# Outputs in the buffers of the relu results, inverse decays in the buffers of the inputs, and a new written-out order: gated linear attention and an MLP mixer on one core

## The chip, the core and the metric

The kernel runs on one core of a Trainium2 chip. A core has TensorE (PE; its weight loads are shown apart as PEld), VectorE (DVE), ScalarE (ACT), GpSimd (POOL) and SyncE (SP), and sixteen DMA engines that move data between HBM and the core's memory. Each engine works through its own list of instructions in order and waits where a semaphore tells it to. The metric is the device time of one launch in microseconds (us), as a median of runs.

## What is computed

The inputs are `q`, `k`, `v`, `alpha` of 4 batches x 8 heads x 768 steps x 48, and four weight matrices of a mixer, all fp32. First comes an attention with a decaying state, then, on its result `x` (4 x 768 x 384), a token mixer and a channel mixer:

```python
for t in range(S):
    state = alpha[:, :, t, :, None] * state + np.einsum('bhd,bhe->bhde', k[:, :, t], v[:, :, t])
    y[:, :, t] = np.einsum('bhd,bhde->bhe', q[:, :, t], state)
# x = y with the heads side by side
h  = np.maximum(x.transpose(0, 2, 1) @ w_tok1, 0.0) @ w_tok2
u  = x + h.transpose(0, 2, 1)
out = u + np.maximum(u @ w_ch1, 0.0) @ w_ch2
```

## The kernel before

**Attention.** The 768 steps of a batch are three chunks of 256; four batches make twelve chunks, numbered 0 to 11. For a chunk, `ld_at`, `ld_kt`, `ld_qt`, `ld_vt` load 384 KB each into buffers of the class `in` (L584). ScalarE takes logarithms (`ln`, L637; from chunk 3 on `P` on POOL or VectorE first, L628, then `ln1`, `lnP`), TensorE sums them (`cum`, `cumw`), and ScalarE makes the decay `E` (L683, L676) and its inverse `IE` (L687, L679). `qq` and `kk` (L700) multiply q by E and k by IE; from chunk 3 on `q0r` (L696) and `k0a` (L692) go ahead of them. `trq` and `trk` transpose them on TensorE (L712), and `evq`, `evk` evict the results; from chunk 6 on the transposes are DMAs of the SP queue, `dq` and `dk` (L725), with `pq` behind. `vb` casts v (L746 on VectorE and POOL, L745 on ScalarE), and `vs`, `ka`, `kb`, `kc` are half-tile copies at the same lines. `G` multiplies keys and queries in narrow blocks of 48 rows, `mask` (L770) keeps the causal half, `K` forms the state's increment, `s` or `sa` and `sm` (L837, L841, L844) update the state `ss`, `ia`, `ib` and `y` give the output, and `x` (L745, L746) evicts it. The two `hf` halves of a chunk are numbered 0 and 1: `mask1_2` is the second mask of chunk 2.

**Mixer.** For each batch `t1` (L878) and `ht` are the first token product and its relu, `t2` (L883) and `u` (L887) the second one and the sum with x. u is transposed into `ut`, in batch 0 by TensorE (`up`, L894) and an eviction, later by DMAs of the SP queue (`ux`, L729). `c1` (L902) is the first channel product, 24 blocks of three matmuls a batch, `rt` its relu (L873 on ScalarE, L875 on VectorE) into twelve buffers of 128 x 768 bf16. `c2` (L907) is the second, four quarters of three matmuls for each of six output tiles; `o` (L911, VectorE) adds u, and `st` (L624) stores 192 KB of fp32 to HBM, from the SP queue or from ScalarE's. In the last batch the tile 0 is cut into two half tiles (`0h0`, `0h1`).

**What sets the order.** `build` lists the steps with their buffers' classes; a fixed text, `ORDER`, names every step once in the order in which it is issued, with a last letter for its engine (t TensorE, s ScalarE, v VectorE, g POOL, y SP), and `BUFS` gives the buffer number of each value in the order of first use. Each engine gets its steps in this order and never passes one. Steps `f1_...` to `f12_...` are dummy matmuls that keep TensorE going at the start. `shared` (L732) makes POOL and VectorE take turns: a step marked `port` on one of them waits for the last such step on the other. `CLASSES` says how many buffers a class has: a step that writes a buffer waits until the last reader of what was in it is done, and for an output that reader is its store. Before the change, outputs have a class `o` of three buffers and IE one of two.

## Time and profile before

| what | before |
|---|---|
| median of 3 runs | 162.97 us (162.54 to 163.51) |
| span of the profiled execution, first to last instruction | 160.5 us |
| TensorE busy in the span | 154.6 us (96%) |
| VectorE, ScalarE, POOL busy | 114.9, 97.8, 80.8 us |
| read from HBM, written | 25.17 MB, 4.72 MB |

The profile is of one execution on the chip; the runs' times are of the whole launch, so 2.5 us of the median lie outside the span. The profiled execution has no time of its own in the records besides its span; 160.5 + 2.5 us stands for it. A row of the timeline has the start, the busy time, the engine, the line, the operation and how many of them were merged; in brackets stands how long the engine was idle before and what released it. A row of a group has busy time and the mean duration of one in ns, and then the idle time before them. A row of waits has the total, how often, and the longest. A row of a stretch has, for each of the five engines, its busy time and the number of its instructions, then the granted clock of TensorE, the share of the DMA engines and GB/s. "issue" is time in which an engine waited for nothing that the profile shows.

### The profile page before, as it was taken

The page shows a single profiled execution, that of the slowest core. Times are in us where ns is not written, and L with a number is a line of the kernel's source. Part 1 is how long each engine was busy: PE and PEld are TensorE (multiplying, and loading weights), DVE is VectorE, ACT ScalarE, POOL GpSimd, SP SyncE. Part 2 cuts the span into 40 slices and gives each one's busy share as a digit, 9 for nine tenths or more (in the row PEclk, how much of TensorE's full clock was granted, in tenths as well). Part 3 has the DMA queues.
Part 4 walks back from the last instruction along what each step waited for, and adds up shares of the span by engine and source line. Part 5 has one row for each costly group of instructions (what it writes and reads, how often), then busy time and mean ns, then how long its engine had stood idle before and what let it go on. Part 6 is the DMA issues. An engine that isn't in the chain of part 4 may idle for free.

```text
span 160.5 us, 3971 instructions
## 1 busy us (share of the span) xinstructions
PE 154.6 (96%) x1563; PEld 97.1 (60%) x1563; DVE 114.9 (72%) x206; ACT 97.8 (61%) x179; POOL 80.8 (50%) x94
## 2 busy tenths in 40 slices
PE   7999989999999999999999999999999999999992
PEld 2545565766667676666667666566567665665661
DVE  6099994979889787989969758795886762464222
ACT  3789999998899955897563583269832203343000
POOL 5205897695973649389778852699523000000000
PEclk9999999999999999999999999999999999999999
DMA  4999999999999999999989999989701235111133
GB/s 122 320 324 317 317 374 311 339 333 306 316 347 324 275 278 272 210 228 319 241 202 298 239 315 204 217 196 134 196 21 62 87 79 169 49 49 53 49 129 116
DMA packets 76130, 35.05 MB, mean 218 GB/s; under 512 B 70352, under 2 KB 74320, under 8 KB 76112
## 3 DMA queue, kind: packets, MB, share of 16 engines
q1 hardware_dynamic: 73808, 31.76, 74.1%
q10 hardware_dynamic: 2304, 3.05, 5.3%
q8 instruction: 12, 0.20, 0.5%
q14 instruction: 6, 0.05, 0.1%
HBM read 25.17 MB, written 4.72 MB: 186 GB/s over the span
## 4 chain that ended last, share of the span: by engine, by line
PE 61%; DMA 12%; DVE 6%; ACT 6%; SPq 6%; POOL 4%; issue 3%; DVEq 0%; POOLq 0%
PE ps L907 22%; PE ps L902 21%; PE ps L643 11%; DMA in<-in_v_dram 6%; SPq L584 6%; DMA out_dram<-o 4%; PE ps L878 3%; PE ps L883 2%; DMA ut<-u 2%; DVE pkk L700 2%; DVE gtm L770 1%; PE ps L712 1%; DVE rt L875 1%; POOL vb L746 1%; POOL pkq L700 1%
## 5 line engine op out<-in xcount | busy, mean ns | idle before, releaser
L907 PE MATMUL ps<-wc,rt 128*128 128x384 bf16 (+1 forms) x300 | 52.4, 319 | 0.0
L902 PE MATMUL ps<-ut,wc 128*128 128x384 bf16 x288 | 50.3, 326 | 0.1
L902 PEld LDWEIGHTS <-wc 128*128 128x128 bf16 x288 | 27.1, 98 | 17.9 <-DMA ut<-u 0.6
L907 PEld LDWEIGHTS <-rt 128*128 128x128 bf16 x300 | 27.8, 98 | 16.0
L873 ACT ACTIVATE rt<-ps 128x384 bf16<-128x384 f32 x47 | 21.4, 492 | 23.6 <-PE ps L902 23.3
L875 DVE TENSOR_SCALAR rt<-ps 128x384 bf16<-128x384 f32 x49 | 25.6, 551 | 9.1 <-PE ps L902 8.9
L770 DVE TENSOR_TENSOR gtm<-ps,mk 128x1024 bf16<-128x1024 f32 x24 | 28.5, 1218 | 3.1 <-PE ps L643 2.8
L911 DVE TENSOR_TENSOR o<-ps,u 128x384 f32<-128x384 f32 (+1 forms) x25 | 13.2, 536 | 12.6 <-PE ps L907 10.1
L700 POOL TENSOR_TENSOR pkk<-in,IE 128x768 bf16<-128x768 f32 x8 | 14.5, 1817 | 3.3 <-DVE ss L844 2.3
L745 ACT CAST x<-ps 128x384 bf16<-128x384 f32 x20 | 9.2, 479 | 11.1 <-PE ps L643 9.5
L887 DVE TENSOR_TENSOR u<-ps,x 128x384 bf16<-128x384 f32 x24 | 12.0, 550 | 3.1 <-PE ps L883 2.5
L746 POOL CAST vb<-in 64x384 bf16<-64x384 f32 (+1 forms) x14 | 8.3, 594 | 10.4 <-DMA in<-in_v_dram 4.7
L692 POOL TENSOR_TENSOR in<-in,in 128x384 f32<-128x384 f32 x8 | 8.0, 1000 | 10.5 <-DVE u L887 3.8
L643 PE MATMUL ps<-rt 128*128 128x512 bf16 (+1 forms) x29 | 12.1, 515 | 1.1 <-DVE rt L541 1.1
L745 ACT CAST vb<-in 64x384 bf16<-64x384 f32 (+1 forms) x18 | 11.4, 634 | 0.8 <-DMA in<-in_v_dram 0.3
L700 POOL TENSOR_TENSOR pkq<-in,E 128x768 bf16<-128x768 f32 x6 | 10.9, 1818 | 0.6 <-DMA tpk<-pkq 0.3
L878 PE MATMUL ps<-x,wt 128*128 128x384 bf16 x48 | 11.0, 325 | 0.0
L844 POOL TENSOR_TENSOR ss<-tmp,E 128x384 bf16<-128x384 f32 x10 | 8.3, 833 | 4.2 <-DVE in L628 3.9
L841 DVE TENSOR_TENSOR tmp<-ps,ss 128x384 f32<-128x384 f32 x16 | 8.8, 552 | 1.8 <-PE ps L643 0.6
L883 PE MATMUL ps<-ht,wt 128*128 128x384 bf16 x48 | 9.1, 326 | 0.0
L643 PE MATMUL ps<-vb,gtm 128*128 128x48 bf16 x192 | 8.2, 183 | 0.2 <-DVE gtm L770 0.2
L643 PE MATMUL ps<-tpq,tpk 48*64 48x128 bf16 (+1 forms) x288 | 7.9, 218 | 0.4 <-POOL tpq L746 0.3
(94 smaller groups left out, 207.6 us busy)
## 6 DMA issues: line engine op xcount, KB each, us to landing
in<-in_alpha_dram SPq DMA_DIRECT2D x12, 384.0 KB, 5.1
in<-in_v_dram SPq DMA_DIRECT2D x12, 384.0 KB, 5.6
in<-in_k_dram SPq DMA_DIRECT2D x12, 384.0 KB, 5.2
in<-in_q_dram SPq DMA_DIRECT2D x12, 384.0 KB, 5.5
in<-in_moe_w_ch_dram SPq DMA_DIRECT2D x12, 384.0 KB, 5.9
...
```

Source lines behind the costliest of these rows:

```text
L643: return self.pe.matmul(out, lhsT=lhsT, rhs=rhs, start=start, stop=stop, skip_group_check=True)
L700: self.shared(self.eng[e].tensor_tensor(self.t(dst)[:, :, h0:h1, 0:D], self.t(src)[:, h0:h1].rearrange("p h s d -> p s h d"), bass.AP(tens ...
L745: return self.act.copy(d, s)
L770: self.nc.vector.tensor_tensor(self.t(gtm)[:, hf, :, :], self.pair(gp).rearrange("p a (j t) -> p (a j) t", t=128), bass.AP(tensor=m.tensor ...
L873: self.act.activation(d, s, AF.Relu)
L875: self.nc.vector.tensor_scalar_max(d, s, 0.0)
L878: self.pe.matmul(self.bank(bank)[:, 0:HD], lhsT=self.wt1[:, kc, m * 128 : m * 128 + 128], rhs=self.t(x), start=(kc == 0), stop=(kc == NS - 1))
L883: self.pe.matmul(self.bank(bank)[:, 0:HD], lhsT=self.wt2[:, kc, i * 128 : i * 128 + 128], rhs=self.t(hts[kc]), start=(kc == 0), stop=(kc = ...
L887: self.nc.vector.tensor_tensor(self.t(u)[:, i % 3], self.bank(bank)[:, 0:HD], self.t(x), ALU.add)
L902: self.pe.matmul(self.bank(bank)[:, 0:HD], lhsT=self.wc1[:, kc, mc * 128 : mc * 128 + 128], rhs=self.t(ut)[:, 3 * half : 3 * half + 3, kc, ...
L907: self.pe.matmul(self.bank(bank)[:, 0 : cz - ca], lhsT=self.t(rts[mc][0])[:, i * 128 : i * 128 + 128], rhs=self.wc2[:, mc, ca:cz], start=( ...
L911: self.nc.vector.tensor_tensor(self.t(o)[:, ca:cz], self.bank(bank)[:, 0 : cz - ca], self.t(u)[:, i % 3, ca:cz], ALU.add)
```

## The change

The classes `IE` and `o` go. Their values keep their names but take buffers of `in` and `rt`, through `ALIAS`; `t` returns such a buffer as a flat tile (for IE) or as fp32 (for an output, 128 x 384 in the same bytes as 128 x 768 bf16). The number of bytes is the same. All of `ORDER` and `BUFS` is replaced, and with them the engine of some steps, the fillers and the place of the stores.

```diff
     def val(self, cls, name=""):
-        return Val(cls, name)
+        return Val(ALIAS.get(cls, cls), cls)
...
-    "in": 19,
-    "la": 2, "lf": 2, "E": 3, "IE": 2, "pkq": 2, "pkk": 3, "vb": 3,
-    "tpk": 4, "tpq": 2, "gtm": 2, "tmp": 2, "ss": 4, "kt": 1, "x": 9, "ht": 3, "u": 4, "ut": 2, "rt": 20, "o": 3,
+    "in": 21,
+    "la": 2, "lf": 2, "E": 3, "pkq": 2, "pkk": 3, "vb": 3,
+    "tpk": 4, "tpq": 2, "gtm": 2, "tmp": 2, "ss": 4, "kt": 1, "x": 9, "ht": 3, "u": 4, "ut": 2, "rt": 23,
 }
+ALIAS = {'o': 'rt', 'IE': 'in'}
...
     def t(self, v):
-        return self.T[v.cls][v.buf]
+        t = self.T[v.cls][v.buf]
+        if v.name == v.cls:
+            return t
+        if v.cls == "rt":
+            return t[:, :].bitcast(F32)
+        return t.rearrange("p h t d -> p (h t d)")
```

The beginning of the order, up to the first `c1`:

```diff
-ld_at1y ld_at0y ln1s ln0s f8_cumw1t f1_cumw1t cumw1t IE1s cumw0t IE0s ld_vt0y E0s vb0g vs0_0g vs1_0v ld_kt0y kk0v
-f8_trk0t f1_trk0t trk0t E1s ld_qt0y qq0v ka0s kb0s kc0v f1_trq0t trq0t ld_kt1y kk1v K0t evq0s s0_0v ld_vt1y vb1s
-f1_trk1t trk1t ld_at2y evk0v ln2s f2_G0_0t G0_0t ld_qt1y ka1g sa1_0v f4_cumw2t cumw2t mask0_0v vs0_1s kb1g kc1g vs1_1s
-K1t sm1_0g qq1v sa0_1v sm0_1v G1_0t ld_kt2y IE2s E2s trq1t evq1s ib0t mask1_0v f3_y1_0t y1_0t y0_0t evk1v G0_1t sa1_1v
-ld_qt2y x1_0s mask0_1v G1_1t ld_vt2y x0_0s vb2s kk2g trk2t kc2s ldw_wt10y qq2g cw_wt10s f2_ia1t ia1t mask1_1v evk2s
-trq2t ld_at3y vs1_2g ldw_wt11y evq2v ib1t y1_1t y0_1t vs0_2g ldw_wt21y sm1_1g P3g K2t sa0_2v sm0_2g x0_1s t1_0_0_0t
-f1_G0_2t G0_2t ldw_wt20y G1_2t cw_wt20g t1_0_1_0t mask0_2v x1_1s t1_0_1_1t ld_at4y ld_kt3y t1_0_1_2t lnP3s cum3t
-cw_wt11s IE3s ia2t y0_2t x0_2s t1_0_0_1t t1_0_0_2t E3s t1_0_0_3t mask1_2v t1_0_1_3t ib2t y1_2t ldw_wc14y t1_0_1_4t
-x1_2s t1_0_0_4t f1_t1_0_1_5t t1_0_1_5t ht_0_1v P4g cw_wt21s t1_0_0_5t ht_0_0s f3_t2_0_0t t2_0_0t t2_0_1t u_0_0v ln13s
-r13s ldw_wc13y t2_0_2t u_0_1v t2_0_3t u_0_2v t2_0_5t lnP4s t2_0_4t u_0_3v u_0_5v u_0_4v up_0_0t cw_wc14s cw_wc13s
-ldw_wc15y up_0_1t ld_qt3y k0a3g kk3g cum4t trk3t cw_wc15g ut_0_0v up_0_2t ut_0_2v ut_0_1s c1_0_11_0t c1_0_8_0t IE4s
...
+ld_kt0y ld_at0y ln0s f12_cumw0t f2_cumw0t cumw0t ld_at1y ln1s ld_qt0y E0s qq0v cumw1t IE0s kk0v IE1s E1s f2_trq0t
+trq0t evq0s ld_kt1y kk1v trk0t evk0v ld_at2y ln2s ld_qt1y kb0s qq1v f3_trk1t trk1t G1_0t evk1v ld_vt0y vb0s ka0g kc0g
+G0_0t cumw2t vs0_0s trq1t ld_vt1y vb1g vs1_0g mask0_0v mask1_0v ld_kt2y IE2s kk2v evq1s f4_K0t K0t E2s f1_G1_1t G1_1t
+vs0_1g s0_0v ib0t ka1v mask1_1v ld_qt2y sa1_0v qq2g y0_0t y1_0t f3_G0_1t G0_1t mask0_1v vs1_1s kb1s kc1s sm1_0g K1t
+sa0_1v trq2t trk2t x1_0s ia1t ldw_wt10y cw_wt10s x0_0s ldw_wt21y cw_wt21g evk2v evq2s y0_1t x0_1v f3_G0_2t G0_2t
+sm0_1g sa1_1v ib1t y1_1t ld_vt2y vb2s mask0_2v G1_2t kc2g t1_0_0_0t vs0_2s K2t ldw_wt11y ld_at3y x1_1s vs1_2s sm1_1g
+t1_0_0_1t ia2t sa0_2v cw_wt11g t1_0_0_2t mask1_2v t1_0_0_3t ld_qt3y ldw_wt20y ln13s t1_0_1_0t r13s t1_0_1_1t y0_2t
+ldw_wc15y sm0_2g ib2t y1_2t t1_0_1_2t t1_0_1_3t x0_2s t1_0_1_4t x1_2s t1_0_0_4t ldw_wc14y t1_0_0_5t P3g lnP3s
+t1_0_1_5t ht_0_1s cum3t ht_0_0v cw_wt20g t2_0_1t E3s u_0_1v t2_0_3t u_0_3v t2_0_0t u_0_0v t2_0_2t t2_0_5t cw_wc15s
+t2_0_4t up_0_0t cw_wc14s IE3s u_0_2v q0r3g qq3g up_0_1t trq3t u_0_5v u_0_4v up_0_2t ldw_wc13y ut_0_1v cw_wc13g ut_0_0s
+c1_0_9_0t evq3s c1_0_10_0t ld_kt3y k0a3v kk3g rt_0_9_0s ut_0_2v c1_0_10_1t rt_0_10_1v ld_vt3y vb3s vs0_3g kb3s ld_at4y
```

Its end, with the second channel product of the last batch:

```diff
-rt_3_9_0v rt_3_4_1s c1_3_5_1t st_1_0y c1_3_9_1t rt_3_9_1s st_2_3s c2_3_2_0t rt_3_5_1v rt_3_10_1v c2_3_2_1t c2_3_2_2t
-c2_3_2_3t c1_3_8_1t rt_3_8_1s o_3_2v c1_3_11_1t rt_3_11_1s c2_3_5_0t c2_3_5_1t rt_3_7_1v c2_3_5_2t c2_3_5_3t c2_3_3_0t
-c2_3_0h1_0t st_3_2s c2_3_0h1_1t c2_3_3_1t c2_3_0h1_2t c2_3_0h1_3t o_3_0h1v st_3_0h1s o_3_5v c2_3_1_0t st_3_5s
-c2_3_3_2t c2_3_3_3t c2_3_4_0t o_3_3v st_3_3y c2_3_4_1t c2_3_4_2t c2_3_4_3t o_3_4v c2_3_1_1t c2_3_1_2t c2_3_1_3t o_3_1v
-st_3_4s c2_3_0h0_0t c2_3_0h0_1t c2_3_0h0_2t c2_3_0h0_3t o_3_0h0v st_3_0h0y st_3_1s
...
+c1_3_7_0t rt_3_7_0v rt_3_5_0v rt_3_10_0v c1_3_9_0t rt_3_5_1v c1_3_3_0t rt_3_3_0s c1_3_0_0t o_2_1v c1_3_1_0t rt_3_1_0v
+c1_3_0_1t rt_3_0_1s st_0_1s c1_3_2_1t c1_3_11_0t c1_3_4_0t rt_3_4_0s c1_3_4_1t c1_3_8_1t c1_3_3_1t rt_3_0_0s
+c2_3_0h0_0t rt_3_2_1v rt_3_9_0v c1_3_6_0t rt_3_6_0v c2_3_2_0t rt_3_11_0v c2_3_0h0_1t c2_3_2_1t c2_3_0h0_2t c2_3_0h0_3t
+o_3_0h0v c2_3_2_2t c2_3_2_3t c2_3_1_0t c2_3_1_1t st_1_2y c2_3_1_2t c2_3_1_3t o_3_1v st_3_1y rt_3_3_1s rt_3_4_1s
+c2_3_5_0t rt_3_8_1s c2_3_4_0t c2_3_4_1t c2_3_4_2t c2_3_5_1t c2_3_4_3t o_3_4v st_3_4s c2_3_5_2t c2_3_5_3t st_2_2y
+st_2_0y o_3_5v st_3_5s o_3_2v st_0_3y c2_3_3_0t c2_3_3_1t c2_3_3_2t c2_3_0h1_0t st_3_2s st_2_4s st_2_1s c2_3_3_3t
+o_3_3v st_3_3y c2_3_0h1_1t c2_3_0h1_2t c2_3_0h1_3t st_3_0h0s st_2_5s o_3_0h1v st_3_0h1y
```

And the stretch of the new order between the token product and the channel product of batch 1:

```diff
+x1_5v t1_1_0_5t ht_1_0v t1_1_1_4t t1_1_1_5t c2_0_1_1t o_0_0v lnP6s cum6t ht_1_1s t2_1_2t u_1_2v t2_1_0t u_1_0v t2_1_5t
+t2_1_1t t2_1_3t u_1_1v IE6s u_1_3v ld_kt8y ln17s t2_1_4t u_1_4v r16s u_1_5v c2_0_1_2t c2_0_4_0t P8g lnP8s E6s
+c2_0_4_1t c2_0_4_2t c2_0_4_3t k0a6g P7g kk6g kb6v ld_qt6y q0r6v k0a8v ld_vt6y vb6s vs0_6v qq6v ld_qt7y ux_1_0y lnP7s
+ux_1_1y r17s q0r7g c2_0_1_3t o_0_1v o_0_4v cum7t IE7s cum8t E8s IE8s E7s c1_1_2_0t rt_1_2_0s c1_1_9_0t rt_1_9_0s
+c1_1_11_0t rt_1_11_0s kk8v c1_1_9_1t rt_1_9_1s c1_1_4_0t ld_vt7y ld_qt8y qq7v c1_1_11_1t rt_1_11_1v c1_1_0_0t
```

95 lines of the change are left out of this document (44 added, 51 removed), and 22 rows, old and new, of the table BUFS.

## The prediction

> **What bounds the kernel now.** I read the page first (span and busy shares), then the busy time of the stretch from 32 us on, then what TensorE's weight loads (PEld, which run ahead of the matmuls and so meet every wait first) waited for in it.
>
> ```profile
> span 160.5 us, 3971 instructions
> PE 154.6 (96%) x1563; PEld 97.1 (60%) x1563; DVE 114.9 (72%) x206; ACT 97.8 (61%) x179; POOL 80.8 (50%) x94
> ```
> ```profile
> 32.00:157.50 125.50, 124.95 (x1246) 80.27 (x1244) 91.05 (x154) 71.22 (x139) 62.37 (x64) 1.00 0.75 200
> ```
> ```profile
> PEld L643 <- issue: 1.5, 5, 0.3
> PEld L902 <- DMA ut<-u: 0.6, 2, 0.5
> PEld L643 <- DVE tpk L746: 0.3, 1, 0.3
> PEld L643 <- DVE o L911: 0.3, 1, 0.3
> PEld L643 <- DMA tpk<-pkk: 0.3, 1, 0.3
> PEld L712 <- issue: 0.3, 1, 0.3
> ```
>
> From 32.0 to 157.5 TensorE works 124.95 of 125.5 us at a granted clock of 1.00. Its loads wait 3.3 us in all there (the six rows), and 1.8 of that is "issue", the switch into a block of narrow matmuls, which has no releaser. What a better order could take away after 32 us is at most the 0.6 + 0.3 + 0.3 + 0.3 = 1.5 us, and 0.55 by the busy column; I use 1.1 us between the two. The change adds and removes no matmul of the work itself. So the time is: when the first matmul of ch1 of batch 0 starts, then the fixed work behind it, then PE's waits, then the tail behind the last matmul. I read each.
>
> The start is set by VectorE:
>
> ```profile
> 8.33 0.35 DVE L746 CAST vb<-in 64x384 bf16<-64x384 f32 x1 [4.26 <-POOL vb L746]
> ...
> 23.17 2.36 DVE L770 TENSOR_TENSOR gtm<-ps,mk 128x1024 bf16<-128x1024 f32 x2
> 26.88 0.56 DVE L875 TENSOR_SCALAR ht<-ps 128x384 bf16<-128x384 f32 x1 [1.36 <-PE ps L878]
> 28.27 2.88 DVE L887 TENSOR_TENSOR u<-ps,x 128x384 bf16<-128x384 f32 x6 [0.83 <-PE ps L883]
> 31.06 0.55 DVE L746 COPY ut<-ps 128x768 bf16<-128x768 bf16 x1
> ```
> ```profile
> 31.76 4.55 PE L902 MATMUL ps<-ut,wc 128*128 128x384 bf16 x27
> ```
>
> VectorE runs without a gap from 8.33 to 23.17 + 2.36 = 25.53 us, which is the end of mask1_2, the last mask of the third attention chunk. Behind it stand x1_2, the last matmuls of tok1, the two ht, tok2 with the six adds of u, and the evictions of ut (the last ends 31.06 + 0.55 = 31.61); ch1 begins at 31.76, which is 6.23 us after the mask.
>
> The loads are the second limit there:
>
> ```profile
> 4.28 0.84 ACT L637 ACTIVATE la<-in 128x768 bf16<-128x768 f32 x1 [2.19 <-DMA in<-in_alpha_dram]
> 5.47 0.84 ACT L637 ACTIVATE la<-in 128x768 bf16<-128x768 f32 x1 [0.35 <-DMA in<-in_alpha_dram]
> ...
> 7.45 0.81 ACT L687 ACTIVATE IE<-ps 128x768 f32<-128x768 f32 x1 [0.32 <-PE ps L643]
> ```
> ```profile
> 6.91 1.39 POOL L746 CAST vb<-in 128x768 bf16<-128x768 f32 x2 [4.11 <-DMA in<-in_v_dram]
> ...
> 30.16 0.88 POOL L746 CAST wc<-in 128x768 bf16<-128x768 f32 x1 [0.36 <-DMA in<-in_moe_w_ch_dram]
> ```
>
> Four instructions that waited for data date the transfers: the 1st at 4.28, the 2nd at 5.47, the 3rd at 6.91, the 22nd (wc15) at 30.16, so one takes (30.16 - 4.28) / 21 = 1.23 us. Its cast ends at 31.04, before the ut eviction at 31.61: data are not last, but only 0.6 us behind.
>
> **The change part by part.**
>
> *The shared classes.* IE is now a view of an `in` buffer and an output tile the first half of an `rt` buffer. No instruction is added; 19 + 2 and 20 + 3 buffers are the 21 and 23 of the new classes. Cost of the views: nothing. What they buy is that a store need no longer come soon after its add, and the new list puts it off. The other aim, instruction fetches, has a trace in the chain, a stand of POOL that nothing releases:
>
> ```profile
> 39.15 0.88 issue
> ```
>
> TensorE waits for nothing there (no row of PEld above is that long), so what it can give back is inside the 1.1 us.
>
> *The order up to the last mask.* Both lists give VectorE 21 instructions up to mask1_2. Four leave it (vs1_0, kc0, sm0_1, evq2) and four others come (kk2, ka1, evk2, x0_1).
>
> ```profile
> L700 DVE TENSOR_TENSOR pkk<-in,IE 128x768 bf16<-128x768 f32 x2 | 1.9, 957 | 0.1
> ...
> L746 DVE COPY tpk<-ps 128x1024 bf16<-128x1024 bf16 x2 | 1.4, 680 | 0.0
> L746 DVE COPY tpq<-ps 128x1024 bf16<-128x1024 bf16 x1 | 1.3, 1305 | 0.0
> L844 DVE TENSOR_TENSOR ss<-tmp,E 128x384 bf16<-128x384 f32 x1 | 0.6, 558 | 0.0
> ...
> L746 DVE CAST vb<-in 64x384 bf16<-64x384 f32 x1 | 0.4, 355 | 4.3 <-POOL vb L746 4.3
> L746 DVE COPY pkk<-pkk 64x384 bf16<-64x384 bf16 x1 | 0.3, 255 | 0.0
> ```
> ```profile
> L746 DVE CAST x<-ps x4: 546/557/558, 60.4 to 124.7; 128x384 bf16<-128x384 f32 x4
> ```
>
> Gone: 355 + 255 + 558 + 1305 = 2.47 us. Come: 957 + 255 (ka1 is the same copy as kc0) + 680 + 557 = 2.45 us. The run of VectorE stays 25.53 - 8.33 = 17.2 us. So only its beginning and its gaps count.
>
> Beginning: the first instruction is now qq0, which needs E0. at0 is the second transfer as before (5.47), its Ln and the matmuls of cumw0 end at 7.45 where IE0 began before; but the list puts ln1 ahead of E0 on ScalarE, and at1 is now third, at 6.91. So ln1 runs 6.91 to 7.75, E0 (0.81) to 8.56, and qq0 starts at 8.6 against 8.33: +0.27.
>
> Gaps: evq2, 1.3 us, now stands on ScalarE behind qq2, which is on POOL and there behind ka1.
>
> ```profile
> 15.95 0.62 PE L712 MATMUL ps<-idn,pkq 128*128 128x128 bf16 x8
> ...
> 18.61 1.82 POOL L700 TENSOR_TENSOR pkq<-in,E 128x768 bf16<-128x768 f32 x1
> ```
>
> Adding the rows up along VectorE, ka1 ends near 18.0, so qq2 near 19.8, its transposes 0.62 later, and evq2 (behind two x evictions) near 22.5; mask0_2 needs it, and VectorE gets there at 23.2. That fits. The next, sa0_2, needs sm1_1 from POOL, near 24.1, and vs1_0, vs0_1 and qq2 on POOL alternate with kk2 and ka1 on VectorE, where each has to wait for the one before (`shared`). Without any gap mask1_2 would end at 8.6 + 17.2 = 25.8; with what these alternations cost I take 26.2, an estimate. The bounds are 25.5 (all gaps vanish and E0 isn't late) and 27.0 (qq2 alone, 1.82 us, half uncovered). Chain: **+0.7 us**, from 0 to +1.5.
>
> Behind mask1_2 the same steps follow with the same engines' rows, so 6.2 us: ch1 at 32.4. The weights are not late: the new order has all three weight pieces of that half among the first 21 transfers, so 4.28 + 20 x 1.23 = 28.9, and the POOL cast of wc13 stands behind qq3 (1.82), to end near 31.4. If that cover is gone, each 0.1 us costs 0.1.
>
> *Work ahead of ch1.* Of TensorE's real work, the new list has trq3 ahead of the first ch1 matmul instead of trk3 (both eight transposes) and cum4 behind it.
>
> ```profile
> L643 PE MATMUL ps<-la,u 128*128 128x384 bf16 x18 | 4.9, 329 | 0.1
> ```
>
> 4.9 / 18 = 0.27 us, and the small matmuls of cum4 make it 0.3: **+0.3 us** to do after the start.
>
> *From 32 us to the last matmul.* Same work, as many blocks of narrow matmuls (nine). Of the waits, one (the 0.5 under `ut<-u`) comes from SP, where a store stood ahead of ux_2_1; in the new list SP has one store before the last batch's transposes. New ones: rt_3_7, rt_3_9 and rt_3_10 now take buffers of outputs, but their stores stand some ten blocks of matmuls, about 5 us, ahead in the lists; so nothing. I take **0**, from -1.1 to +1.5 (one new wait at each of the three batch changes as long as the 0.5 above).
>
> *The tail.* Here the change has its clear price.
>
> ```profile
> 157.04 0.34 ACTq L624 DMA_DIRECT2D out_dram<-o  x1
> 157.44 0.36 DVE L911 TENSOR_TENSOR o<-ps,u 128x192 f32<-128x192 f32 x1 [0.43 <-PE ps L907]
> 157.83 0.33 SPq L624 DMA_DIRECT2D out_dram<-o  x1
> ```
> ```profile
> DMA  7399300199600000006991000079806800000000
> ...
> q10 hardware_dynamic: 504, 0.63, 22.8%
> q1 hardware_dynamic: 288, 0.30, 10.9%
> ```
>
> ```profile
> 133.97 10.72 PE ps L902 x66
> ```
>
> The second fence is the DMA from 153.0 us to the end, 7.5 us in forty slices of 0.19: the two queues are busy 33.7% of it, 2.53 us, for 0.93 MB, so a store of 192 KB holds the sixteen engines 0.53 us. The store issued at 157.04 shows in the slice that begins at 153 + 26 x 0.1875 = 157.9, so its data move 0.85 us after the issue. Before, the last two stores are issued 0.8 us apart and hardly touch. A matmul of 384 columns takes 10.72 / 66 = 0.162 us (third fence, from the chain that ended last), a tile of ch2 twelve of them, 1.95, and a half tile 0.98. In the new list o_3_2 comes behind o_3_5 on VectorE, though its matmuls are done 8.8 us before the end, and on ScalarE five stores stand behind it: st_3_2, st_2_4, st_2_1, st_3_0h0, st_2_5. Behind the matmuls of o_3_5 come a tile and a half tile, 2.93 us, to TensorE's end T; so o_3_5 (0.56, with the lag of the last matmul) ends near T - 2.2, o_3_2 near T - 1.6, and the five issues of 0.34 us each reach T + 0.1. With st_3_5, st_3_3 and st_3_0h1 that is 6 x 0.53 + 2 x 0.27 = 3.7 us of transfer, which can't begin before T - 2.2 + 0.85 = T - 1.3 and so ends near T + 2.4. Before, the last one is issued at 157.83, T + 0.4, and by the same count ends at T + 1.6. **+0.8 us**, from +0.3 (the adds come earlier) to +1.2 (o_3_0h1, which now waits for the landing of st_3_5, is late; nothing is queued behind it). By the Trainium skill, DMA: Bandwidth & Descriptors, section Issuing engines are not separate DMA queues, DMAs started by different engines run on the same 16 engines and interleave. If the two queues were apart instead, the tail would cost nothing and the sum would be 1.0, 164.0 in all; no row of this trace has two stores at once on both queues.
>
> **Sum.** 0.7 + 0.3 + 0 + 0.8 = +1.8 us on the span of 160.5: 162.3. Around the span lie 162.97 - 160.5 = 2.5 us to the median of the three runs, which stay: **164.8 us**.
>
> **The rivals.**
>
> *PE's waits go (faster).* SP, freed of stores, issues loads and transposes in time, and the start loses nothing because the alternations between POOL and VectorE fit: work +0.3, waits -1.1 and tail +0.3 make -0.5; with nothing in the tail and the chain 0.3 shorter it is -1.1. I take -1.0, so 162.0. It decides if ch1 starts by 31.7 and the waits after it are under 0.5 us. For it: SP's store ahead of ux_2_1. Against: VectorE's sum is unchanged and E0 is later. 0.14.
>
> *Gains and losses cancel.* Chain 0 to +0.3, tail +0.3: 163.4. 0.20.
>
> *A new wait in the steady part.* ux_1_0 must land before the first ch1 of batch 1, and behind the two matmuls of tok2 for its last add stand two more such pairs, six quarter tiles of ch2 and two cum, 0.65 + 6 x 0.49 + 0.6 = 4.2 us, less 0.7 for the add, so 3.5, against 3.1 to 3.8 us from issue to landing of the same transfer in batch 2:
>
> ```profile
> DMA to landing us min/median/max: 3.1/3.5/3.8
> ```
>
> A late SP or a full queue there adds 0.5 to 2 us: 166.3. 0.16.
>
> *The clock falls.* The new list fills TensorE's idle start with fewer dummy matmuls. The Trainium skill, TensorE: Matmul & The Clock Gate, section What's actually happening, says that after an idle window of about 3.4 us the clock halves. By the rows, the twelve matmuls of tok2 would then cost twice their 1.95 us, so 166.7. The trace has 1.00 throughout, and I see no idle stretch of over 1.5 us. 0.04.
>
> **How the numbers follow.** Forecast with its own range (164.0 to 165.6) 0.46, the four rivals 0.54. About 0.5% (0.8 us) is what a measurement of this kernel can tell from no change. Faster by more: 0.14; within: 0.20; slower: 0.46 + 0.16 + 0.04 = 0.66. The range 162.3 to 167.0 leaves out some of the first rival and the worst of the third, about 0.2.
>
> **What would show it.** Right: mask1_2 of the third chunk ends at 26 or later; the first ch1 matmul at 32.0 to 33; PE's waits after it 1 to 2 us; four stores or more landing after the last matmul, and the span ending over 3.6 us behind it. Wrong: ch1 before 31.8, or a tail of 3.1 us as now (160.5 - 157.4), or waits of TensorE over 3 us after 33.

## The result and the profile after

The changed kernel takes 163.87 us as the median of 17 runs, the kernel before 162.80 in as many beside it: the ratio is 1.0054, with a 95% interval of 1.0030 to 1.0077. It is slower, as forecast, but by half of what the sum gave: 0.9 us by the ratio (1.07 between the medians) and not 1.8. One of the 17 runs of the changed kernel took 541.24 us, and the ratio leaves it out.

In every run of both kernels the launch takes 1.7 us longer than its span. The profiled execution of before, with 160.5, was one of the shorter ones: the median of 162.80 less 1.7 is a span of 161.1. So 0.8 of the 2.5 us that the forecast put around the span is scatter between executions. The new kernel's profiled execution spans 161.7 us.

First the page of the new kernel, then the stretch that answers to the one shown of before, then what TensorE's weight loads waited for in it:

```profile
span 161.7 us, 3962 instructions
...
PE 154.5 (96%) x1556; PEld 97.0 (60%) x1556; DVE 116.1 (72%) x209; ACT 98.2 (61%) x182; POOL 73.7 (46%) x88
```
```profile
32.00:158.50 126.50, 125.11 (x1249) 80.14 (x1247) 92.43 (x156) 72.05 (x145) 56.05 (x58) 1.00 0.79 197
```
```profile
PEld L650 <- issue: 1.8, 6, 0.4
PEld L719 <- POOL pkk L707: 0.5, 1, 0.5
PEld L650 <- DVE rt L918: 0.5, 1, 0.5
PEld L909 <- issue: 0.4, 1, 0.4
PEld L650 <- DMA tpk<-pkk: 0.3, 1, 0.3
PEld L650 <- DVE tpk L753: 0.3, 1, 0.3
PEld L650 <- DMA in<-in_alpha_dram: 0.3, 1, 0.3
PEld L650 <- DVE rt L882: 0.2, 1, 0.2
PEld L650 <- DVE ht L882: 0.2, 1, 0.2
```

(The lines of the new kernel are seven higher than before's: L707 is `qq` and `kk`, L777 the mask, L909 `c1`, L914 `c2`, L918 `o`, L631 the stores.) The clock is 1.00 throughout. The waits are 4.5 us against 3.3, and more of them are single late partners: POOL, VectorE's adds, a load of alpha.

Now VectorE at the start, in the order of time:

```profile
8.74 0.96 DVE L707 TENSOR_TENSOR pkq<-in,E 128x768 bf16<-128x768 f32 x1 [4.67 <-ACT E L690]
9.62 1.82 DVE L707 TENSOR_TENSOR pkk<-in,in 128x768 bf16<-128x768 f32 x2
11.35 0.68 DVE L753 COPY tpk<-ps 128x1024 bf16<-128x1024 bf16 x1
...
24.12 1.22 DVE L777 TENSOR_TENSOR gtm<-ps,mk 128x1024 bf16<-128x1024 f32 x1
26.69 0.56 DVE L882 TENSOR_SCALAR ht<-ps 128x384 bf16<-128x384 f32 x1 [1.36 <-PE ps L885]
27.82 2.88 DVE L894 TENSOR_TENSOR u<-ps,x 128x384 bf16<-128x384 f32 x6 [0.58 <-PE ps L890]
```
```profile
31.32 1.95 PE L909 MATMUL ps<-ut,wc 128*128 128x384 bf16 x11
```

The first `qq` waits for E as forecast, and later than forecast (8.74, not 8.6). But the last mask ends at 24.12 + 1.22 = 25.34, not at 26.2, and ch1 begins at 31.32, 0.44 us earlier than before and not 0.7 later.

At the other end, ScalarE's store issues, VectorE's last two adds, and the DMA from 154 us to the end, 7.7 us in forty slices of 0.1925:

```profile
154.73 3.84 ACTq L631 DMA_DIRECT2D out_dram<-rt  x7
```
```profile
157.31 0.56 DVE L918 TENSOR_TENSOR rt<-ps,u 128x384 f32<-128x384 f32 x1 [1.18 <-PE ps L914]
158.06 0.36 DVE L918 TENSOR_TENSOR rt<-ps,u 128x192 f32<-128x192 f32 x1 [0.19 <-PE ps L914]
```
```profile
DMA  9997000079900699999999999999999910000000
...
q10 hardware_dynamic: 1008, 1.28, 44.9%
q1 hardware_dynamic: 507, 0.58, 20.8%
```

TensorE's last matmul ends at T = 158.02. The DMA is full without a gap from slice 13 (156.5, T - 1.5) to slice 32 (160.2, T + 2.2), and the span ends 3.69 us behind T. Before it was 3.12.

The two profiled executions add up, with T at 157.41 before. The work is an estimate: the number of matmuls of each shape, times the median step from the start of one to the start of the next. How the narrow matmuls are priced moves both columns alike, so the differences are firmer than the sums.

| term | forecast | before | after | difference |
|---|---|---|---|---|
| first ch1 matmul | +0.7 | 31.76 | 31.32 | -0.44 |
| work behind it (matmuls at their own pace) | +0.3 | 120.0 | 120.3 | +0.29 |
| T less ch1 less that work: waits | 0 | 5.6 | 6.4 | +0.77 |
| T to the end of the span | +0.8 | 3.12 | 3.69 | +0.57 |
| span | +1.8 | 160.5 | 161.7 | +1.2 |

Two terms were right, one (the start) had the wrong sign and one (the waits) was taken as zero. One profile of each can't say which of these differences belong to the order and which to the execution; the experiments can.

### The profile page after: what moved, and what is told of

It reads as the page before. It is cut to its first block, busy times and chain, and to the rows that moved or that the text cites. A ratio compares the mean times of both kernels' runs of the same rounds, so it can differ in the third digit from the quotient of the medians.

```text
span 161.7 us, 3962 instructions
## 1 busy us (share of the span) xinstructions
PE 154.5 (96%) x1556; PEld 97.0 (60%) x1556; DVE 116.1 (72%) x209; ACT 98.2 (61%) x182; POOL 73.7 (46%) x88
## 4 chain that ended last, share of the span: by engine, by line
PE 58%; DMA 12%; DVE 5%; POOL 5%; SPq 4%; issue 2%; ACT 1%; POOLq 0%; DVEq 0%
PE ps L909 24%; PE ps L914 19%; DMA in<-in_v_dram 7%; PE ps L650 6%; PE ps L890 4%; PE ps L885 3%; DMA in<-in_alpha_dram 3%; SPq L591 3%; DMA ut<-u 2%; DVE tmp L848 2%; PE ps L719 1%; DVE rt L918 1%; POOL ss L851 1%; POOL pkk L707 1%; SPq L631 1%
## 5 line engine op out<-in xcount | busy, mean ns | idle before, releaser
L914 PE MATMUL ps<-wc,rt 128*128 128x384 bf16 (+1 forms) x300 | 53.1, 320 | 0.0
L909 PE MATMUL ps<-ut,wc 128*128 128x384 bf16 x288 | 50.1, 326 | 0.3 <-DMA ut<-u 0.3
L880 ACT ACTIVATE rt<-ps 128x384 bf16<-128x384 f32 x54 | 24.3, 493 | 23.2 <-PE ps L909 23.0
L909 PEld LDWEIGHTS <-wc 128*128 128x128 bf16 x288 | 27.2, 98 | 17.7 <-issue 0.5
L914 PEld LDWEIGHTS <-rt 128*128 128x128 bf16 x300 | 27.7, 98 | 15.8
L882 DVE TENSOR_SCALAR rt<-ps 128x384 bf16<-128x384 f32 x42 | 21.8, 553 | 11.6 <-PE ps L909 11.5
L777 DVE TENSOR_TENSOR gtm<-ps,mk 128x1024 bf16<-128x1024 f32 x24 | 28.7, 1218 | 1.6 <-PE ps L650 0.9
L918 DVE TENSOR_TENSOR rt<-ps,u 128x384 f32<-128x384 f32 (+1 forms) x25 | 13.1, 535 | 8.7 <-PE ps L914 8.0
L752 ACT CAST vb<-in 64x384 bf16<-64x384 f32 (+1 forms) x21 | 13.9, 663 | 1.6 <-DMA in<-in_v_dram 1.2
L650 PE MATMUL ps<-rt 128*64 128x384 f32 (+1 forms) x22 | 10.6, 599 | 1.1 <-DVE rt L542 1.1
L707 POOL TENSOR_TENSOR pkq<-in,E 128x768 bf16<-128x768 f32 x6 | 10.9, 1817 | 1.5 <-DVE kt L753 0.8
L707 POOL TENSOR_TENSOR pkk<-in,in 128x768 bf16<-128x768 f32 x6 | 10.9, 1818 | 1.1 <-DVE in L699 1.0
L703 POOL TENSOR_TENSOR in<-in,lf 128x384 f32<-128x384 f32 x7 | 7.0, 998 | 7.8 <-DVE pkq L707 3.5
L707 DVE TENSOR_TENSOR pkq<-in,E 128x768 bf16<-128x768 f32 x6 | 5.7, 954 | 4.7 <-ACT E L690 4.7
L753 POOL CAST vb<-in 64x384 bf16<-64x384 f32 (+1 forms) x12 | 6.4, 529 | 5.6 <-DVE vb L753 3.9
L650 PEld LDWEIGHTS <-tpk 48*64 48x64 bf16 (+1 forms) x288 | 5.8, 102 | 4.2 <-issue 2.1
```

The source lines that it names most:

```text
L650: return self.pe.matmul(out, lhsT=lhsT, rhs=rhs, start=start, stop=stop, skip_group_check=True)
L707: self.shared(self.eng[e].tensor_tensor(self.t(dst)[:, :, h0:h1, 0:D], self.t(src)[:, h0:h1].rearrange("p h s d -> p s h d"), bass.AP(tens ...
L752: return self.act.copy(d, s)
L777: self.nc.vector.tensor_tensor(self.t(gtm)[:, hf, :, :], self.pair(gp).rearrange("p a (j t) -> p (a j) t", t=128), bass.AP(tensor=m.tensor ...
L880: self.act.activation(d, s, AF.Relu)
L882: self.nc.vector.tensor_scalar_max(d, s, 0.0)
```

## The experiments

All change `ORDER` and `BUFS` alone (and, where said, the classes); the letter at a step's end is its engine. The ratio is to the kernel before, with its 95% interval; "tail" is the time from the last matmul to the end of the span in the profiled execution. The ratio is estimated from runs taken beside each other, and it needn't be the quotient of two medians: for w_act_o those would give 162.49 / 162.97 = 0.997.

| kernel | median us | ratio | ch1 at | tail |
|---|---|---|---|---|
| after | 163.87 | 1.0054 (1.0030 to 1.0077) | 31.32 | 3.69 |
| again | 163.89 | 1.0058 (1.0028 to 1.0087) | 31.83 | 3.71 |
| v_views | 162.94 | 0.9988 (0.9957 to 1.0018) | 31.59 | 3.10 |
| v_late | 163.98 | 1.0061 (1.0023 to 1.0100) | 31.61 | 3.91 |
| h_start2 | 165.02 | 1.0138 (1.0092 to 1.0184) | 31.69 | 3.13 |
| h_rest2 | 166.56 | 1.0239 (1.0192 to 1.0286) | 31.92 | 3.69 |
| t_tail | 163.76 | 1.0051 (1.0014 to 1.0087) | 31.50 | 3.15 |
| t_late | 165.73 | 1.0163 (1.0123 to 1.0202) | 31.65 | 5.68 |
| s_early | 165.95 | 1.0184 (1.0137 to 1.0232) | 31.58 | 3.16 |
| w_pool | 164.15 | 1.0072 (1.0037 to 1.0107) | 31.23 | 3.71 |
| w_ux | 166.55 | 1.0213 (1.0158 to 1.0267) | 31.82 | 3.70 |
| all3 | 164.86 | 1.0133 (1.0081 to 1.0185) | 31.52 | 3.15 |
| w_sp | 167.21 | 1.0251 (1.0207 to 1.0294) | 31.45 | 3.71 |
| w_act | 163.30 | 1.0034 (1.0003 to 1.0064) | 31.37 | 3.69 |
| w_act_tail | 162.89 | 0.9990 (0.9958 to 1.0022) | - | 3.16 |
| w_act_o | 162.49 | 0.9999 (0.9972 to 1.0026) | 31.40 | 3.14 |

### The classes alone: v_views

```diff
-    "in": 19, ... "IE": 2, ... "rt": 20, "o": 3,
+    "in": 21, ... "rt": 23,
+ALIAS = {'o': 'rt', 'IE': 'in'}
 ORDER: as before
```

> Only the shared classes, with the order, engines and fillers of before; each output and each inverse decay gets a buffer of its own in the larger class, as before. If the views cost nothing (my theory: the whole difference is the order), the time is that of before within 0.3 us, ratio 0.998 to 1.002, first ch1 matmul near 31.8 and 3.1 us from the last matmul to the end. Rival, that the shared memory itself costs (other addresses, added waits): slower by 0.5 us or more, ratio 1.003 or above.

The ratio is 0.9988, and ch1 and the tail stand where they stood before. Shared buffers with the old order cost nothing and give nothing that shows; all of the change is its order.

### Each of them once more: again, b_again

> The changed kernel once more, on the same chip as the pieces: ratio 1.003 to 1.008, ch1 at 31.2 to 31.4, tail 3.6 to 3.8. If ch1, the waits or the tail differ by over 0.3 us from the first profile, single profiles are too rough to read the pieces from.

> The kernel before once more, for a second profile: ch1 at 31.6 to 31.9, sum of PE's waits behind it 4.6 to 5.3 us, tail 3.1. If the sum differs by over 1 us from the first profile's, the 0.8 us more of the changed kernel is inside what single profiles scatter.

The changed kernel spans 163.3 us in its second profile against 161.7 in the first, before 161.0 against 160.5 (with ch1 at 31.71 and a tail of 3.11). The tail is the same to 0.02 us each time. What moves between executions of one program is the start (31.32 and 31.83) and the waits in the middle: 1.0 us more in the second profile of the changed kernel, 0.5 us more in that of before, so that the second pair differs by 1.3 us where the first differs by 0.77. By the first expectation's own limit of 0.3 us, one profile is too rough to read the start or the waits from; the tail can be read from it.

In this execution ScalarE stands near 113 us, where it did not in the first. Here are ScalarE's rows, and then the rows of the chain that ended last:

```profile
111.16 0.46 ACTq L631 DMA_DIRECT2D out_dram<-rt  x1
111.67 0.49 ACT L880 ACTIVATE rt<-ps 128x384 bf16<-128x384 f32 x1
112.89 0.34 ACTq L631 DMA_DIRECT2D out_dram<-rt  x1
113.28 0.87 ACT L880 ACTIVATE rt<-ps 128x384 bf16<-128x384 f32 x2 [1.12 <-DMA tpk<-pkq]
```
```profile
106.76 6.12 DMA tpk<-pkq
112.87 0.02 issue
112.89 0.34 ACTq L631
113.23 0.05 issue
113.28 0.88 ACT rt L880 x2
114.16 0.04 issue
114.20 1.62 PE ps L909 x9
```

The relu ends at 112.16, and the next entry of ScalarE's list, the store `st_1_0`, is issued only at 112.89; the relus behind it are 1.1 us late, and TensorE waits 0.71 for them at 114.20. The chain and the bracket name what the store waited for: the landing of `dq10`, the transposing DMA that SP issued at 106.76 and that landed at 112.87. `st_1_0` neither reads nor writes what `dq10` moves. The trace shows one semaphore on this issue, the one with which `dq10` reports its landing, so the two transfers share it. It is the same in each profile in which `st_1_0` stands there: it is issued 0.02 us after `dq10` has landed, at 111.95 in t_tail, 111.38 in t_late, 111.94 in w_pool, 114.27 in h_rest2 and 115.31 in w_ux, and TensorE then waits 0.64, 0.40, 0.37, 0.79 and 0.74 us; in all3 and w_sp it is issued so too, at 114.77 and 115.10, and TensorE doesn't wait for it. In the first profile `dq10` took 4.83 us and had landed at 110.92, before `st_1_0` came up at 111.03: no stand. So the order is open to it, and executions differ in how late `dq10` lands. (A fetch of instructions on the queue q14 lies near the stand in some of these profiles. It lies among the relus in the first profile and in w_act too, at 110.7 and 111.5 us, and none of their relus stands for it.)

### Start and rest apart: h_start, h_rest, h_start2, h_rest2

h_start and h_start2 take the new list up to the first `c1` and the old one behind; h_rest and h_rest2 the other way round.

> The new order up to the first ch1 matmul, then the order of before (six buffers renumbered). If start, middle and tail add up as read: ch1 begins at 31.3 as in the changed kernel, then 0.3 us more work (cum4 and trk3 stand behind it instead of trq3), PE's waits and the tail as before: last matmul at about 157.3, time 0.1 to 0.2 us below before, ratio 0.998 to 1.000. Rival, that the earlier ch1 is paid back by later attention and weights: PE's waits between 32 and 60 us grow by 0.4 or more, ratio 1.001 to 1.005.

> The order of before up to its first ch1 matmul, then the new order (four buffers renumbered). If the parts add up: ch1 at 31.8, waits and tail of the changed kernel, so 0.15 us above the changed kernel: ratio 1.006 to 1.010. Rival, that the new start is the cause of the new waits: waits as in before, ratio 1.003 or less.

Both cuts were bad. Steps that the other list has ahead of its first `c1` (`cum4` and `trk3` in one, `trq3` in the other) were left in front of it, and TensorE waited there, 2.2 us for `kk3` in h_start and 4.0 us for `qq3` in h_rest. ch1 began at 36.3 and 36.1 us, the ratios are 1.035 and 1.037, and they say nothing of the question. In the second pair these steps go behind the first blocks of `c1`:

```diff
 new list up to c1_0_9_0, then the old one, with
+c1_0_11_1t cum4t ... c1_0_7_1t trk3t ... evk3s
 (h_rest2: old list up to c1_0_11_0, then the new one, with)
+c1_0_6_1t trq3t evq3s ... c1_0_11_0t G0_3t mask0_3v G1_3t
```

> The new order up to the first ch1 matmul, then the order of before, with cum4 put behind its third block of ch1 and trk3 behind its ninth (their data come later in the new list of loads, and in the first cut of this kind they held the first ch1 matmul at 36.3). If the new start is harmless and the loss sits in the rest: ch1 at 31.3 to 31.8, tail 3.1, ratio to before 0.997 to 1.002. Rival, that the new start costs later (data and attention of chunk 3 come late): PE's waits between 32 and 50 us 0.5 us or more above the 1.0 of before, ratio 1.003 or more.

> The order of before up to its first ch1 matmul, then the new order, with trq3 behind the fifth block of ch1 and the narrow products of chunk 3 a few blocks later. If the loss sits in the rest: ch1 near 31.7, PE's waits after it and the tail (3.7) as in the changed kernel, ratio 1.004 to 1.010. Rival, that the start is the cause: ratio 1.002 or less.

The seams cost more than what was to be measured. In h_start2 TensorE waits 1.2 us there for a weight cast on ScalarE:

```profile
38.16 2.61 PE L909 MATMUL ps<-ut,wc 128*128 128x384 bf16 x15 [1.19 <-ACT wc L752]
```

Both ratios lie above what theory and rival gave, so the times don't split the change. The profiles do: with the new start and the old rest the tail is 3.13, with the old start and the new rest 3.69, and the late waits near 88 and 115 us go with the new rest. Start and tail are each where their own list puts them.

The start can be averaged over all kernels whose cut is not in it. With the new start (twelve profiles) the last mask ends at 25.55 on average and ch1 begins 5.98 to 5.99 us behind it, at 31.53; with the old one (five profiles) at 25.49, 6.23 us behind it, 31.72. So the new start is 0.2 us earlier.

### The tail: t_tail, t_late, v_late

```diff
 t_tail, on after:
+st_0_1s st_1_2y st_2_2y st_2_0y st_0_3y st_2_4y st_2_1y st_2_5y c1_3_2_1t
+o_3_0h0v st_3_0h0s c2_3_2_2t c2_3_2_3t o_3_2v st_3_2s c2_3_1_0t
 t_late, on after:
+st_3_0h0s st_2_5s st_1_2s st_2_2s st_2_0s st_0_3s o_3_0h1v
 v_late, on v_views:
+st_3_4s st_2_4s st_2_1s st_2_5s st_2_2s c2_3_0h0_0t
```

> The changed kernel, but the outputs leave as soon as they are there: o_3_2 and st_3_2 right behind their matmuls, st_3_0h0 behind its add, and st_1_2, st_2_2, st_2_0, st_0_3, st_2_4, st_2_1, st_2_5 ahead of st_3_1 on SP. If the clump of late stores is what made the tail 3.7 us instead of 3.1: tail back to 3.1 to 3.2, time 0.5 to 0.6 us below the changed kernel, ratio to before 1.001 to 1.003. Rival, that the tail is long for another reason or the stores only move their cost into the last batch: tail still 3.5 or more, or PE waits in the last 25 us, ratio 1.004 to 1.007.

> The changed kernel with four more stores (st_1_2, st_2_2, st_2_0, st_0_3) put behind the last one on ScalarE. If a store that is late costs its 0.53 us of transfer one for one, in the profile and in the time of a launch: tail 3.7 + 4 x 0.53 = 5.8 us, time 2.1 us above the changed kernel, ratio 1.016 to 1.022. Rival, that the end of a launch hides late stores (which would be why the early ones gained nothing that could be measured): tail 5.8 in the profile, but ratio 1.010 or less.

> The order of before with the shared classes, and four stores of batch 2 (st_2_4, st_2_1, st_2_5, st_2_2) held until behind st_3_4: the late stores alone, without the rest of the new order. By the same count five stores of 0.53 us stand from 1.0 us before the last matmul on: tail 3.1 + 0.7 to 0.9, ratio to before 1.002 to 1.007 (with shared classes alone it was 0.999). Rival, that the tail is hidden: tail as said, ratio 0.997 to 1.001.

Late stores count in full. Four more of them on the new order lengthen the tail from 3.69 to 5.68 us and the ratio from 1.0054 to 1.0163, 1.8 us; four on the old order take the tail from 3.10 to 3.91 and the ratio from 0.9988 to 1.0061, 1.2 us. In t_late each late store costs about 0.5 us in the tail, which is the 0.53 us that one holds the sixteen engines.

But t_tail, which makes the tail as short as before's (3.15), gains nothing that shows: 1.0051. Either the tail does not matter after all, which t_late and v_late speak against, or something in the middle hides the gain (its profile has the wait near 113 us, 0.64 long), or it is the scatter: by the two intervals the difference from 1.0054 is uncertain by 0.4%, 0.7 us, which is more than the 0.54 us of tail. The last pair below bears on it.

### The waits between 60 and 92 us: w_pool, w_ux, all3, w_sp

The first of them is the place that the third rival named. Rows of the chain that ended last:

```profile
59.63 4.83 DMA in<-in_v_dram
64.46 3.73 DMA ut<-u
...
68.23 3.59 PE ps L909 x21
```

The transposes of u for batch 1 are issued at 64.46, behind loads of v and q, and the first lands 3.7 us later; the first ch1 of batch 1 waits for it, its loads 0.4 us and TensorE itself 0.28. The next ones, near 86 and 89 us, go back to loads of alpha that SP issues at 79.5 and 81.8 us:

```profile
81.76 4.22 DMA in<-in_alpha_dram
...
86.36 0.71 issue
87.07 0.84 POOL ss L851
...
89.02 0.89 PE ps L650 x20
```

`P10` on POOL waits for the second one, and the state update queued behind it (`sm0_7`, 87.07) holds TensorE at 89.02, by 0.37 us. (The 0.71 of "issue" in the chain is no stand: `P10` itself runs on POOL from 86.11 for 1.00 us.) Three mends, one each, and the first two with t_tail as all3; of w_ux and w_sp only SP's steps are shown:

```diff
 w_pool:
-kc8g P10g
+sm0_7g P10g
 w_ux:
-ld_qt7y ux_1_0y ux_1_1y
+ux_1_0y ld_qt7y ux_1_1y
 w_sp:
-dk6y dq7y dk8y dk7y ld_vt8y ld_at9y st_0_4y ld_at10y
+dk6y ld_at9y dq7y dk8y ld_at10y dk7y ld_vt8y st_0_4y
```

> The changed kernel with one step moved on POOL: P10 (which waits for a late load) now behind sm0_7, which the state chain needs. If POOL's wait for that load is what held TensorE 0.5 us near 89.0: that wait falls under 0.15 and the last matmul comes 0.3 to 0.5 us earlier, ratio 1.002 to 1.004. Rival, that the place is short of something else and the wait only moves: the sum of PE's waits from 80 to 95 us stays at 1.2 to 1.3 and the time that of the changed kernel, ratio 1.004 to 1.007.

> The changed kernel with one step moved on SP: the transposing DMA ux_1_0 ahead of the load of q for chunk 7. If the load ahead of it in the queue is what made ux_1_0 land 3.7 us after its issue and held the first ch1 matmul of batch 1 by 0.4 us near 68.2: that wait is gone, the last matmul 0.2 to 0.4 us earlier, ratio 1.002 to 1.004. Rival, that the later load then holds chunk 7: a new wait of as much between 68 and 85 us, ratio 1.004 to 1.008.

> The three mends at once on the changed kernel: early stores, P10 behind sm0_7, ux_1_0 ahead of the load of q for chunk 7. If the pieces add: 0.55 + 0.4 + 0.3 us off, so 162.6, ratio 0.997 to 1.001, about before or a little below. Rival, that the removed waits come back elsewhere: ratio 1.002 or more.

> The changed kernel with two loads moved ahead on SP: ld_at9 from behind dk7 and ld_vt8 to just behind dk6, ld_at10 from behind st_0_4 to just behind dk8. In the order of before these two are issued at 69.4 and 72.7 us, in the changed kernel at 79.5 and 81.8. If their lateness makes PE's waits between 80 and 92 us: the sum there falls from 1.3 to 1.6 to the 0.8 of before, 0.4 to 0.8 us off, ratio 0.999 to 1.003. Rival, that the place is short of transfers whatever the order, as when ux_1_0 was moved: the transposes dq7, dk8, dk7 land later and a new wait of 0.5 us or more comes between 76 and 90, ratio 1.004 or more.

None helped, and all3 comes to 1.0133. In w_pool the wait at 89 us goes, and waits of 0.64, 0.32 and 0.34 us stand at 84.5, 86.1 and 91.1 in its place: the rival, the wait only moves. In w_ux the load of q, which in the changed kernel is issued at 61.9 while SP waits for u, is issued at 66.1 and lies between the two transposes; the second one lands 5.1 us after its issue, and ch1 of batch 1 waits 2.2 us (2.1 in all3, which has the same edit). In w_sp `dk7` comes later and TensorE waits 2.6 us for it. In w_ux and w_sp the wait is followed by something else (stretches of w_ux, then of w_sp: busy time of PE and PEld, then the other three engines, the granted clock, DMA, GB/s):

```profile
68.00:71.90 3.90, 1.69 (x16) 0.94 (x14) 1.85 (x4) 2.71 (x7) 1.00 (x1) 1.00 1.02 207
71.90:75.30 3.40, 3.40 (x11) 1.57 (x11) 2.04 (x3) 0.49 (x1) 1.49 (x2) 0.50 1.17 272
75.30:79.00 3.70, 3.70 (x24) 2.25 (x23) 1.69 (x4) 3.33 (x6) 1.92 (x2) 1.00 0.97 205
```
```profile
84.60:88.00 3.40, 3.40 (x13) 1.62 (x11) 2.62 (x5) 0.77 (x2) 2.26 (x4) 0.51 0.88 232
```

TensorE is granted half the clock for 3.4 us, which costs about another 1.7 (an estimate, half of the 3.4). That is how a moved load costs 2%. In all3 the wait is nearly as long and the clock stays at 1.00, so the length of the wait does not decide it alone. In each profile the changes of the clock lie whole multiples of 3.41 us apart. Cut into stretches of this length, so that each change falls on a border, the twenty profiles have six stretches in which TensorE works less than half the time (0.56 to 1.67 us: one each in w_ux, w_sp, w_act_tail and h_rest, two in h_start), and each of the six is followed by a stretch at 0.50. In every other stretch TensorE works 1.81 us or more (the least is in s_early, from 67.4 us), and none of these is followed by one. The wait of w_ux falls into one stretch, which is left with 1.20 us of work; that of all3 lies across two, with 2.58 and 2.14. In w_act_tail two waits of 0.94 and 1.19 us, close together, left 1.49 us of work in one stretch, and that was enough. The Trainium skill, TensorE: Matmul & The Clock Gate, section What's actually happening, puts the fall after a window of about 3.4 us of idleness; here the length of the stretches agrees, and TensorE did not have to be idle for all of one.

### Where the stores of the middle stand: s_early, w_act

s_early puts every store of the first three batches soon behind its add, on ScalarE, and mends the tail; w_act only moves five stores of the changed kernel from ScalarE to SP.

```diff
 s_early, for example:
+o_0_3v c2_0_0_3t st_0_5s ld_at6y
+qq7v c1_1_11_1t st_0_1s st_0_4s rt_1_11_1v
 w_act:
-... st_1_5s ... st_0_0s ... st_1_4s ... st_0_5s ... st_1_0s ...
+ld_vt10y st_1_5y st_0_0y st_0_5y ... dq10y st_1_4y st_1_0y pq10s
```

> The changed kernel with every store of batches 0 to 2 put, on ScalarE, eight matmul blocks behind its add at the latest, and o_3_2, st_3_2 and st_3_0h0 early: the delay of the stores, which the shared buffers allow, is undone, all else of the new order stays. If the delayed stores cost in two places, the tail and ScalarE's dense stretch of relus at 105 to 115 us: tail 3.1, no wait of PE over 0.3 us near 113, ratio 1.000 to 1.003. Rival, that the early stores cost as much by taking transfers from the loads: PE's waits between 60 and 95 us grow by 0.5 or more, ratio 1.004 or more.

> The changed kernel with five of the delayed stores (st_1_5, st_0_0, st_0_5, st_1_4, st_1_0) taken from ScalarE, where they stand between the relus of batch 2, and put on SP around dq10. If their issues on ScalarE (0.34 us each) make TensorE's wait of 0.5 to 0.9 us near 113 to 115: that wait is gone, 0.4 to 0.9 us off, ratio 0.999 to 1.003. Rival, that ScalarE stands there for its instructions (a fetch is seen at 110.9 to 111.7 in each of those profiles): the wait stays over 0.4, ratio 1.004 to 1.008.

s_early is 1.8% slower than before, though its tail is 3.16 and the wait near 113 is gone: TensorE waits 1.2 us at 68.7 for a logarithm on ScalarE and 1.2 at 78.9 for an eviction there, and ScalarE itself stood before each for a transfer, 2.7 us for a load of v and 1.8 for a transposing DMA. That fits the rival, that early stores take transfers from the loads; that it was the stores that made these two transfers late is not shown by itself. So stores are not better early in general; putting them off had a use.

w_act has no wait near 113: `dq10` lands at 113.12, later than in the second profile of the changed kernel, and yet the five relus run ahead of it without a stand, since no store stands between them. Only `pq10`, which reads what `dq10` brings, waits for it, 0.59 us. So the wait near 113 was that of `st_1_0`, and the rival, that ScalarE stands there for its instructions, is out. The ratio, 1.0034 with the tail of the changed kernel, lies between the two ranges.

### Both mends: w_act_tail, w_act_o

w_act_tail is w_act with the edit of t_tail; w_act_o is w_act with only `o_3_2`, its store and the store of `0h0` early:

```diff
 w_act_o, on w_act:
+o_3_0h0v st_3_0h0s c2_3_2_2t c2_3_2_3t o_3_2v st_3_2s c2_3_1_0t
```

> The new order with both single mends that lost nothing: five stores of the middle go from ScalarE's queue to SP around dq10, and the seven late stores and o_3_2 go early again. Theory (tail counts one for one in the time, and its mend alone gained nothing since the same stores on ScalarE and the full queues cost as much in the middle): tail 3.1 to 3.2, the new order's wait near 113 under 0.3, median 0.4 to 0.6 us under that with the five stores alone (163.30), ratio 0.999 to 1.001. Rival (stores cost the same wherever they are put, since the middle pays what the tail saves): ratio 1.003 to 1.005 with TensorE's last matmul later by 0.5 us.

> As the last, but the seven late stores stay late: of the tail only o_3_2 and its store and the store of the first half tile 0 go early. Theory: the tail is set by the five stores behind o_3_2 on ScalarE; three of them stay, so it shrinks by two stores of 0.53 and 0.27 us at most, to 3.1 to 3.4, and nothing moves in the middle: ratio 1.000 to 1.002. Rival (stores cost the same wherever they are put): no middle is touched here, so the tail alone gains, and it and the last kernel differ by 0.3 us or more in this one's favour.

0.9990 and 0.9999: both are at the time of before, and the interval of w_act_o (0.9972 to 1.0026) lies apart from that of the changed kernel (1.0030 to 1.0077). w_act_o in profile, from 154 us to its end in forty slices of 0.165, and ScalarE near the place of the wait:

```profile
DMA  7000005994007999999999994499796000000000
...
q10 hardware_dynamic: 720, 0.98, 39.9%
q1 hardware_dynamic: 337, 0.35, 14.6%
```
```profile
109.52 2.29 ACT L880 ACTIVATE rt<-ps 128x384 bf16<-128x384 f32 x5 [1.28 <-PE ps L909]
111.71 1.34 ACT L752 COPY tpq<-tpk 128x1024 bf16<-128x1024 bf16 x1
```

The five relus run on without a stand, as in w_act. (Of w_act_tail's profile only the tail and the middle can be compared: TensorE's clock was 0.50 from 18.4 to 21.8 us in that execution, and ch1 began at 33.8.) The rival, that stores cost the same wherever they are put, would have left w_act_tail at 1.003 to 1.005; that is outside its interval. Its second sign, w_act_o ahead of w_act_tail by 0.3 us or more, is met by the medians (0.40) and not by the ratios, so that part stays undecided. No version beats the kernel before by more than its interval.

## Why the prediction was right or wrong, step by step

**Slower, through the tail: right.** The direction and the clearest term held. The forecast had the last stores' data run from T - 1.3 to T + 2.4; they ran from T - 1.5 to T + 2.2. The tail grew by 0.57 us in place of 0.8, since the transfers began 0.2 us earlier, inside the bounds of 0.3 to 1.2. The two queues share one bandwidth. The GB/s of the changed kernel's tail, with a fifth of the bytes of its last stretch on SP's queue, and then of v_late's from 154 us to its end, where SP's queue has 8%:

```profile
GB/s 399 391 407 287 8 0 0 0 271 399 335 16 0 247 423 367 399 383 375 399 391 367 391 355 347 407 407 399 383 391 363 323 32 0 0 0 0 0 0 0
```
```profile
GB/s 0 298 395 369 62 0 0 0 0 0 0 0 255 386 395 404 386 360 386 413 369 378 395 395 378 369 386 356 400 404 395 97 0 0 0 0 0 0 0 0
```

The full slices of the last stretch average 385 and 386, so stores on the second queue added no bandwidth, and the tail came as counted with one. So the doubt about queues that are apart is settled against it, as the Trainium skill, DMA: Bandwidth & Descriptors, section Issuing engines are not separate DMA queues, has it.

**The chain at the start: this is the step that failed.** "The run of VectorE stays 25.53 - 8.33 = 17.2 us. So only its beginning and its gaps count." With 0.4 us for the gaps that is 17.6 us. The beginning was right: +0.41 us in the first profile, where +0.27 was said, and +0.34 on average (8.59 over the twelve profiles with the new start, 8.25 over the five with the old). The run was not. From 8.74 to 25.34 it is 16.6 us in the first profile, and over the twelve it is 16.6 to 17.4, 16.96 on average, though the durations of the 21 instructions sum to 17.7 in both lists. Where one VectorE instruction stands ready behind another, the next one begins 0.08 us before the other ends (9.62 + 1.82 = 11.44, the next row starts at 11.35). Where it is held for something it begins 0.01 to 0.13 us after. In the old list 9 of 20 such steps lack this overlap (one of them only in part), in the new list's first profile 4. The sum of durations is therefore no length of a run, and equal sums don't make equal runs.

The gaps were half right. In the first profile the alternation with POOL left none of more than 0.15 us, but in nine of the twelve `sa0_1` on VectorE waits 0.13 to 0.72 us for `sm1_0`, which stands behind `qq2` on POOL (the longest is in the second profile of the changed kernel, before 21.00 us). Over all twelve that is 0.24 us on average. Without this wait the new run would be 16.7 us on average, 0.5 less than the 17.2 taken for it. The gain in the run balances the late beginning: the mask ends at 25.55 against 25.49, +0.06 and not +0.7. Which of the old list's holds went, and why, was not isolated.

"Behind mask1_2 the same steps follow, so 6.2 us" was off by 0.25 as well: 5.98, to 0.01, in each of the twelve against 6.23. The rows show where: before the six adds of u VectorE waits 0.58 us and not 0.83. The old list has three dummy matmuls ahead of the first `t2` and the new one none; that this is the reason is argued, not tried. Together the start gave -0.2 us where +0.7 was forecast, and ch1 before 31.8 was one of the forecast's own signs of being wrong. That miss of 0.9 us is as large as the whole excess of the forecast. Of the measured 0.9 us, start, work and tail make -0.2 + 0.3 + 0.57, so about 0.2 is left for the waits: the 0.2 that the tail was forecast too high is offset by them.

**Work ahead of ch1: right**, +0.29 for +0.3.

**TensorE's waits: taken as zero, and they are not.** "New ones ... so nothing" looked only at the buffers that outputs now share, and these indeed cost nothing (v_views). What the new list brought was late partners elsewhere: the transposes of u at 68 us, the place and the mechanism of the third rival at 0.3 to 0.4 us in place of 0.5 to 2; alpha loads behind a store on SP's queue; and the shared semaphore that holds ScalarE near 113 us. The first pair of profiles gives +0.77 and the second +1.3, both inside the range of -1.1 to +1.5; the medians leave about 0.2. So "nothing" was too low as a best value. The single places can't be mended one by one (w_pool, w_ux, w_sp), but the five stores on ScalarE were worth about 0.2% and the tail about 0.35% behind them (1.0054, 1.0034, 0.9999). The 0.2%, 0.3 us, fits the wait at `st_1_0`, which is 0 to 0.71 us and 0.42 on average in the five profiles that have the changed kernel's middle as it is (after, again, t_tail, t_late, w_pool). The two steps taken singly are not apart from their neighbours by their intervals; both together are, and with both gone nothing measurable of the loss is left.

**Instruction fetches.** The 0.88 us of "issue" at 39.15 in the chain of before was read as a stand of POOL. It is none: POOL runs `P` (L628) there, from 39.08 for 1.00 us. The chain leaves a step where the next one stops waiting for it, and what follows of the step itself appears as "issue". Neither here nor near 113 us was an engine shown to wait for a fetch.

**The rivals.** That PE's waits go, and that the clock falls, did not happen in the changed kernel; the clock did fall in five experiments (w_ux, w_sp, w_act_tail, h_start, h_rest). "Gains and losses cancel" was the nearest in size, 163.4, and wrong in its reason: the start didn't come out even, it gained.
